# A fused attention, FFN and gated-convolution kernel: batches 2 and 3 row by row, W decode scratch moved, the order replanned

## The chip, the core and the metric

The kernel runs on one core of a Trainium2 chip. A core has five engines, each with its own in-order instruction queue: TensorE (PE, matmuls and weight loads), VectorE (DVE), ScalarE (ACT), GpSimd (POOL) and SyncE (SP), which here only issues DMAs. The metric is the device time of one execution in microseconds. Three runs of the kernel before gave 767.53, 768.31 and 769.16 us, median 768.31.

## The reference

Four batches of 576 positions, 8 heads of 64, model width 512, FFN width 2048:

```
q_rot, k_rot = rotate(q), rotate(k)              # rotary embedding
attn = softmax(q_rot @ k_rot^T / 8)              # per batch and head, 576 x 576
x = heads joined of attn @ v                     # (4, 576, 512)
xn = (x - mean) / sqrt(var + 1e-6) * g_ln
x = x + relu(xn @ w_ch1) @ w_ch2                 # 512 -> 2048 -> 512
gate = sigmoid(causal depthwise conv of x, 5 taps)
out = (gate * (x @ w_val)) @ w_out
```

The weights arrive as 64-bit floats, in 1 MB pieces that are decoded on the chip from their two 32-bit halves. Matmuls that must be accurate split an operand into a high and a low float16 (or two rounded float32) and add three products.

## The kernel before

**Attention.** Work is cut in *score tiles* of 128 queries of one head: 144 of them, 36 for each batch. A tile is: scores on TensorE (`a_scores`, two heads of a pair together), row maximum on VectorE (`a_max`, L478), exponential and a float16 copy on ScalarE (`a_exp` L484, `a_hi` L490), the rest of the float16 split on VectorE (`a_lo`, L495), a DMA transpose issued by SP (`a_turn`, L500), and 14 matmuls with V on TensorE (`a_pv`, L519 and L522). Since 576 is four and a half times 128, the 64 queries left over of both heads of a pair form one tile of their own, the *lead* (its first tile index is `None`). Queries and keys are rotated on VectorE (`mul`, `add`), then split (`hi` on ScalarE, `lo` on VectorE). V is bounded and split as well: absolute sums on ScalarE (`vabs`), one matmul that spreads them (`vsum`), a maximum and a scale on VectorE (`vmax`), then `vhi`, `vlo`, `vturn`.

Batches 0 and 1 go *row by row*: for a row of queries all four head pairs in turn, then the next row, so that a block of 128 positions is complete, in all heads, early. For that the keys of all four pairs stay in SBUF (`kf` for batch 0, `kx0` for batch 1), and queries of a row are loaded and prepared alone (`cuts` lists the rows). Batches 2 and 3 go pair by pair: a pair's keys and all its queries are loaded and prepared together into one buffer of a ring of two (`kq`), and all nine tiles of the pair follow.

**FFN.** When a block of 128 positions is complete, it is normalised (`ln_a` to `ln_d`, transposed by a DMA), and then goes through the FFN in four quarters of the hidden width: `f1` (48 matmuls, L780), `relu` and `hlo`, `f2` (12 matmuls, L808). There are 18 blocks, so 72 `f1` and 72 `f2` steps. `f1` needs W1, which is scaled in four parts of two pieces each; `f2` needs W2, of which the scale is known only when all eight pieces have been decoded.

**Weights.** A 1 MB piece of W is loaded into a scratch buffer (L612), decoded by two ScalarE passes (`p1`, `p0`) and one of VectorE (`p2`, L625), multiplied with itself for a bound (`products`, L641), and, when the scale of its part is known (`conv_max`, `conv_turn`, `conv_scale`), split in two float16 parts (`conv_hi` L679 on ScalarE, `conv_lo` L682 on VectorE, which writes half of `wall`). W1 has three scratch buffers inside `wall`, W2 has two (`kk`), in the space where the ring `kq` lies later. Each `conv_hi` waits for the `conv_lo` before it.

**Last stage.** For pairs of blocks: a transposing DMA, the convolution (`gate_b`), `val` (12 matmuls), `proj` (24), and the store. It begins when the attention buffers are given back.

**Order.** Nothing is ordered at run time. Each piece of work is a `plan.step` with an engine, an assumed duration, a rank, the steps it waits for and the ring buffers it takes or uses. `Plan.run` walks through them with assumed lags (`LAG`) and an assumed DMA rate (`RATE`) and, on each engine, takes the step with the lowest rank among those that can start; that list is the order in which each engine's queue is written. A change of any duration, lag or dependence can so reorder all queues.

Of the kernel before, what the change touches and what calls it, by code (L numbers as in the profile page):

```python
# [27 lines left out]
QS, QK_LEAD_1 = 3, 6  # L28
XT, KQ, RAW, GT, X3, GV = 3, 2, 3, 6, 1, 1
# [125 lines left out]
def kernel(ctx: ExitStack, tc: tile.TileContext, qk, v, g_ln, w_ch1, w_ch2, w_val, conv_w, w_out, rope, eye, out):  # L155
# [40 lines left out]
    kx0 = xpool.tile([128, NP, 2, S], F32R, name="kx0", tag="x1")  # L196
# [27 lines left out]
    ap_k = R(sA, "ap_k", KQ)  # L224
    kk = [ap_k.tile([128, 4 * S], F32, name="kk", tag="kq") for _ in range(2)]
# [59 lines left out]
    attention, early = [], []  # L285
# [4 lines left out]
    def plan_prep(p):  # L290
# [6 lines left out]
        r0 = first[p] - (QK_LEAD_0 if p < NP else QK_LEAD_1 if b < 2 else QK_LEAD)  # L297
# [6 lines left out]
        def vload():  # L304
            st["vt"] = (pool if p < NP else ap_v).tile([128, 10, D], F32, name="vt", tag="vt", bufs=2 if p < NP else 1)
# [50 lines left out]
        for n in ((0,) if two else (1, 0)):  # L356
# [6 lines left out]
            if n:  # L363
                takes = [Buf("kq" if b > 1 else f"kx{pr}" if b else f"kf{pr}")]
                bf["kq"] = takes[0]
            elif b < 2:
                takes = [Buf("qx" if p < NP else "qs" if b else "qf")]
                bf["q"] = takes[0]
            else:
                bf["q"] = bf["kq"]  # L370
# [9 lines left out]
            uses = [bf["raw", n]] + ([bf["q"]] if not n and not takes else [])  # L380
# [709 lines left out]
```

## Time and profile before

| | |
|---|---|
| median of 3 runs | 768.31 us |
| the profiled execution | 765.1 us |
| its span | 763.3 us |
| TensorE busy | 683.1 us, 89% |
| VectorE busy | 621.5 us, 81% |
| ScalarE busy | 454.4 us, 60% |
| DMA moved | 103.60 MB |

The span runs from the first to the last instruction of the profiled execution. What lies around it is 765.1 - 763.3 = 1.8 us. A busy engine is one that executes instructions; matmuls overlap in the pipeline, so a row of matmuls takes less than their number times their mean.

### The profile page before, as it was taken

To read this page: it belongs to the slowest core of one execution; us is meant where nothing else is said; L and a number is where in the kernel's file an instruction comes from. 1 tells how busy PE (TensorE), PEld (TensorE's weight loads), DVE (VectorE), ACT (ScalarE), POOL (GpSimd) and SP (SyncE) were. 2 spreads that over 40 slices of the span, in tenths; PEclk is the share of its full clock that TensorE was granted. 3 is DMA by queue.
4 is the path that set the end of the run, shared out by engine and by line. 5 is a ranking of instruction groups with operands and counts; after the bars stand their busy time and mean duration, and the time that the engine had idled before them with its cause. 6 is when DMAs were issued, how large, how long until landed. Compare 5 with 4: busy or idle time off the path is not lost.

```text
span 763.3 us, 19105 instructions
## 1 busy us (share of the span) xinstructions
PE 683.1 (89%) x7929; PEld 529.0 (69%) x7929; DVE 621.5 (81%) x1257; ACT 454.4 (60%) x778; POOL 16.3 (2%) x40
## 2 busy tenths in 40 slices
PE   2575766789999999999999989999999999999996
PEld 1344645545887777777777767877777887878875
DVE  6889987999889999897787987668779988666525
ACT  5877777787666557776666666464744443333323
POOL 0000000000000000000000100001000000000000
PEclk9977989889999999999999999999999999999999
DMA  8998799754987898689777777768843223301011
GB/s 295 272 249 244 153 244 216 185 126 119 157 138 136 169 186 172 131 170 176 112 149 152 143 139 97 108 114 106 234 70 70 57 56 56 57 29 28 15 56 41
DMA packets 231734, 103.60 MB, mean 136 GB/s; under 512 B 210784, under 2 KB 218976, under 8 KB 231648
## 3 DMA queue, kind: packets, MB, share of 16 engines
q1 hardware_dynamic: 231648, 102.39, 66.4%
q8 instruction: 62, 1.02, 0.6%
q14 instruction: 24, 0.20, 0.1%
HBM read 45.73 MB, written 4.72 MB: 66 GB/s over the span
## 4 chain that ended last, share of the span: by engine, by line
PE 57%; DVE 22%; DMA 13%; ACT 5%; issue 3%; SPq 1%; ACTq 0%; DVEq 0%
PE acc L808 17%; PE hp L780 16%; DMA pT<-p 9%; PE pv L957 6%; PE po L984 6%; PE sc L473 4%; DVE p L495 3%; PE ov L519 3%; DVE nmx L478 3%; PE sc L468 2%; DMA vt<-in_v_dram 2%; DVE wall L682 2%; DVE raw L314 2%; PE ov L522 2%; DVE wall L625 1%
## 5 line engine op out<-in xcount | busy, mean ns | idle before, releaser
L780 PE MATMUL hp<-xT,wall 128*128 128x128 f16 x3456 | 206.0, 220 | 1.6 <-DVE wall L682 1.6
L780 PEld LDWEIGHTS <-wall 128*128 128x128 f16 x3456 | 196.6, 98 | 7.3 <-DVE wall L682 1.8
L808 PE MATMUL acc<-wall,hh 128*128 128x512 f16 x544 | 162.1, 380 | 0.4 <-DVE x L812 0.4
L484 ACT ACTIVATE p<-sc,nmx 128x576 f32<-128x576 f32 x144 | 105.2, 736 | 82.5 <-DVE nmx L478 80.9
L495 DVE SCALAR_TENSOR_TENSOR p<-p,p 128x576 f16<-128x576 f32 x144 | 107.6, 753 | 27.5 <-ACT p L490 27.2
L519 PE MATMUL ov<-vh,pT 128*128 128x65 f16 (+1 forms) x1296 | 93.7, 200 | 27.3 <-DMA pT<-p 17.1
L519 PEld LDWEIGHTS <-pT 128*128 128x128 f16 x1296 | 79.2, 100 | 45.5 <-DMA pT<-p 28.3
L478 DVE TENSOR_REDUCE nmx<-sc 128x1 f32<-128x576 f32 x144 | 105.0, 750 | 4.1 <-PE sc L473 3.6
L808 PE MATMUL acc<-wall,hl 128*128 128x512 f16 x272 | 103.1, 379 | 0.0
L490 ACT ACTIVATE p<-p 128x576 f16<-128x576 f32 x144 | 97.2, 681 | 6.1 <-DMA pT<-p 3.6
L808 PEld LDWEIGHTS <-hh 128*128 128x128 f16 x544 | 48.6, 98 | 51.3 <-issue 2.3
L944 DVE SCALAR_TENSOR_TENSOR gt<-xT,cw,gt 128x256 f32<-128x256 f32 (+4 forms) x192 | 72.1, 413 | 6.6 <-ACT gt L935 4.0
L522 PE MATMUL ov<-vl,pT 128*128 128x64 f16 (+1 forms) x720 | 68.9, 200 | 0.0
L792 ACT ACTIVATE hh<-hp 128x512 f16<-128x512 f32 x68 | 40.1, 590 | 36.7 <-PE hp L780 36.6
L798 DVE SCALAR_TENSOR_TENSOR hl<-hp,hh 128x512 f16<-128x512 f32 x68 | 46.7, 686 | 16.3 <-ACT hh L792 16.2
L522 PEld LDWEIGHTS <-pT 128*128 128x128 f16 x720 | 53.4, 100 | 4.2 <-issue 0.3
L808 PEld LDWEIGHTS <-hl 128*128 128x128 f16 x272 | 26.6, 98 | 32.9 <-DVE hl L798 1.1
L984 PE MATMUL po<-woh,gv 128*128 128x512 f32 x144 | 47.7, 400 | 1.8 <-DVE gv L972 1.4
L957 PE MATMUL pv<-xh,wvh 128*128 128x256 f32 x144 | 44.1, 307 | 0.0
L314 DVE TENSOR_TENSOR raw<-raw,rope_sb 128x1152 f32<-128x1152 f32 (+2 forms) x40 | 39.6, 991 | 4.3 <-DMA raw<-in_qk_dram 4.3
L957 PE MATMUL pv<-xl,wvh 128*128 128x256 f32 x144 | 40.6, 282 | 0.7 <-DVE xl L929 0.7
L957 PE MATMUL pv<-xh,wvl 128*128 128x256 f32 x144 | 40.5, 281 | 0.0
(126 smaller groups left out, 937.6 us busy)
## 6 DMA issues: line engine op xcount, KB each, us to landing
raw<-in_qk_dram SPq DMA_DIRECT2D x24, 576.0 KB, 4.8
wall<-in_moe_w_ch_dram SPq DMA_DIRECT2D x8, 1024.0 KB, 6.5
kk<-in_moe_w_ch_dram SPq DMA_DIRECT2D x8, 1024.0 KB, 6.4
vt<-in_v_dram SPq DMA_DIRECT2D x16, 320.0 KB, 3.6
out_dram<-x SPq DMA_DIRECT2D x18, 256.0 KB, 2.0
raw<-in_qk_dram SPq DMA_DIRECT2D x24, 128.0 KB, 3.1
pT<-p SPq DMA_TRANSPOSE x144, 3.6
r<-in_moe_w_val_dram SPq DMA_DIRECT2D x4, 512.0 KB, 4.7
```

What stands on the lines that cost most here:

```text
L314: nc.vector.tensor_tensor(out=a, in0=a, in1=t, op=ALU.mult)
L478: nc.vector.tensor_reduce(out=nmx, in_=sc[:, :, 0:HS], axis=AX.XY, op=ALU.max, negate=True)
L484: nc.scalar.activation(out=p32.rearrange("p (e n) -> p e n", e=2), in_=sc[:, :, 0:HS], func=ACTF.Exp, bias=nmx)
L490: nc.scalar.activation(out=p16[:, 0], in_=p32, func=ACTF.Copy, scale=P_SCALE)
L495: nc.vector.scalar_tensor_tensor(out=p16[:, 1], in0=p32, scalar=P_SCALE, in1=p16[:, 0], op0=ALU.mult, op1=ALU.subtract)
L519: nc.tensor.matmul(o, pT[:, c], vh[:, 2 * c + hs:2 * c + hs + nh], start=(c == 0), stop=(c == 8))
L522: nc.tensor.matmul(o[..., 0:D], pT[:, c], vl[:, 2 * c + hs:2 * c + hs + nh], start=False, stop=False)
L780: nc.tensor.matmul(hp[:, j], w1[:, u, wl * 512 + o:wl * 512 + o + 128], xT[:, xl * KD + c], start=(i == 0), stop=(i == 3 * KD - 1))
L808: nc.tensor.matmul(st["acc"], lw[:, j], w2[:, f + j, lo * 512:lo * 512 + 512], start=(f + j == 0 and i == 0), stop=(f + j == KF - 1 and i ...
L944: nc.vector.scalar_tensor_tensor(out=gt[:, c0:c1], in0=xT[:, c, HALO + c0 - s:HALO + c1 - s], scalar=col(KT - 1 - s, c), in1=gt[:, c0:c1], ...
L957: nc.tensor.matmul(pv, lw[:, d, c * 128:(c + 1) * 128], rx[:, d], start=(n == 0), stop=(n == 3 * KD - 1))
L984: nc.tensor.matmul(po, lw[:, d, sl], rx[:, d, :], start=(n == 0), stop=(n == 3 * KD - 1))
```

## The change

- Batches 2 and 3 are cut in rows as batches 0 and 1 are (`cuts` by `b % 2`). Their keys lie in `k2`, two tiles of two pairs each in the space of `kk`; each pair's keys are a ring of one (`k20` to `k23`), written for batch 2 and again for batch 3. Their queries use the small ring `qs`.
- W1's scratch: four buffers in `wall` and two in a new tile `xw`, which lies where `kx0` and later the second half of `x` come. W2's: the two `kk` and the same two in `xw`. So `kx0` starts only when the W2 pieces in `xw` are decoded, `k2` when those in `kk` are.
- A `conv_hi` of W1 no longer waits for the `conv_lo` just before it but for the one before that.
- The bounds of V of the four pairs of batch 0 are merged: four absolute sums, four matmuls into one tile, one maximum and one scale for all; their loads have a buffer each (`vt0=NP`).
- `X3` becomes 2 (two buffers for the split block of the last stage), `RATE` 280 in place of 313, the lag of DMA 2.4 in place of 1.9, and several assumed durations change.

On the instructions: the number of matmuls is the same. VectorE has 108 instructions more, ScalarE 24, SP 24 DMAs.

```diff
-XT, KQ, RAW, GT, X3, GV = 3, 2, 3, 6, 1, 1
+T_LAG, RATE, NEAR, AHEAD = 2.4, 280.0, 0.15, 2.0
+XT, KQ, RAW, GT, X3, GV = 3, 2, 3, 6, 2, 1
...
-        if b == 0:
+        if b % 2 == 0:
             cuts = [(c, c + 128, [(0, c), (1, c)]) for c in (0, 128, 256)] + [(384, S, [(None, c4), (0, 384), (1, 384)])]
-        elif b == 1:
+        else:
             cuts = [(0, 192, [(None, c4), (0, 64), (1, 64)])] + [(c, c + 128, [(0, c), (1, c)]) for c in (192, 320, 448)]
-        else:
-            cuts = [(0, S, [(None, c4)] + [(h, f0 + 128 * j) for j in range(4) for h in range(2)])]
...
+        def vsum0():
+            v0["va"] = ps_h.tile([128, NP, 128], F32, name="va0", tag="hp")
+            for j in range(NP):
+                nc.tensor.matmul(v0["va"][:, j], upper(v0["vb"][:, j:j + 1]).to_broadcast([128, 128]), ident, start=True, stop=True)
+
+        def vmax0():
+            vm = pro_x.tile([128, NP], F32, name="vm0", tag="vm0", bufs=1)
+            nc.vector.tensor_reduce(out=vm, in_=v0["va"], axis=AX.X, op=ALU.max)
...
+            v_abs.append(plan.step(ACT, act(640) + 0.09, r, vabs, after=[x0, x1], uses=[vt, vh], row="vabs"))
...
+                x = plan.step(PE, 0.3, R_TINY, vsum0, after=v_abs + [c_c], takes=[hp])
...
+    def k2_start():
+        k2.extend(ap_k.tile([128, 2, 2, S], F32R, name="k2", tag="kq") for _ in range(2))
...
     scratch = (
-        [unit(wfu, a, 4) for a in (18, 22, 26)],
-        [unit(k, 0, 4) for k in kk],
+        [unit(wfu, a, 4) for a in (18, 22, 26, 30)] + [xw[:, 0], xw[:, 1]],
+        [unit(k, 0, 4) for k in kk] + [xw[:, 0], xw[:, 1]],
     )
...
-                    y = plan.step(ACT, act(n) + 0.09, r, lambda a=a: conv_hi(*a), after=[x, chain])
-                    chain = plan.step(DVE, dve(n) + 0.06, r, lambda a=a: conv_lo(*a), after=[y, chain])
+                    y = plan.step(ACT, act(n) + 0.09, r, lambda a=a: conv_hi(*a), after=[x, chains[-1 if w else -2]])
+                    chains.append(plan.step(DVE, dve(n) + 0.06, r, lambda a=a: conv_lo(*a), after=[y, chains[-1]]))
...
+    e_kx = plan.step("", 0, 0, kx_start, after=[p2s[1, 6], p2s[1, 7]])
+    e_k2 = plan.step("", 0, 0, k2_start, after=[p2s[1, 4], p2s[1, 5]])
```

SP's queue around the last W2 loads, before. `kk` rows are W2 pieces, `pT` rows transposes of score tiles, `raw` rows queries or keys, `xT` a normalised block:

```order
L500 DMA_TRANSPOSE pT<-p_1280 128x9x128
L770 DMA_TRANSPOSE xT<-x_1295 128x8x128
L302 DMA raw<-in_qk_dram 128x1152
L500 DMA_TRANSPOSE pT<-p_1322 128x9x128
L612 DMA kk<-in_moe_w_ch_dram 128x2x1024
L500 DMA_TRANSPOSE pT<-p_1339 128x9x128
L500 DMA_TRANSPOSE pT<-p_1443 128x9x128
L612 DMA kk<-in_moe_w_ch_dram 128x2x1024
L500 DMA_TRANSPOSE pT<-p_1464 128x9x128
L302 DMA raw<-in_qk_dram 128x2x192
L500 DMA_TRANSPOSE pT<-p_1564 128x9x128
L612 DMA kk<-in_moe_w_ch_dram 128x2x1024
```

And in the changed kernel, where W2's pieces lie in `kk` and `xw` in turn:

```order
L304 DMA raw<-in_qk_dram 128x2x192
L531 DMA_TRANSPOSE pT<-p_921 128x9x128
L649 DMA kk<-in_moe_w_ch_dram 128x2x1024
L531 DMA_TRANSPOSE pT<-p_942 128x9x128
L304 DMA raw<-in_qk_dram 128x2x192
L649 DMA xw<-in_moe_w_ch_dram 128x2x1024
L531 DMA_TRANSPOSE pT<-p_1031 128x9x128
L531 DMA_TRANSPOSE pT<-p_1064 128x9x128
L304 DMA raw<-in_qk_dram 128x2x192
L649 DMA xw<-in_moe_w_ch_dram 128x2x1024
```

Each piece ends with the last W2 load. Before, 25 score transposes stand ahead of it in the queue, and 3 ahead of the first W2 load; in the changed kernel 16 and 8.

VectorE's queue up to the first W2 piece that is split (`wall<-wall,s`), before. `wn`, `w_m`, `w_r` and `scl` belong to W2's bound and scale, `nmx` and `p` to score tiles, `vl` to V, `raw` to keys and queries:

```order
L478 TENSOR_REDUCE nmx<-sc 128x1
L657 TENSOR_REDUCE wn_1925<-hp 128x1
L147 TENSOR_SCALAR w_m<-wn_1925 128x1
L148 RECIPROCAL w_m<-w_m 128x1
L150 TENSOR_SCALAR w_r<-w_m 128x1
L668 TENSOR_SCALAR s_77<-srt,w_r 128x4
L644 TENSOR_SCALAR scl<-w_r 128x1
L670 TENSOR_SCALAR scl<-scl,smin 128x1
L429 SCALAR_TENSOR_TENSOR vl<-vt,sv,vh 128x640
L322 TENSOR_TENSOR raw<-raw 128x192
L314 TENSOR_TENSOR raw<-raw,rope_sb 128x1152
L682 SCALAR_TENSOR_TENSOR wall<-wall,s_77 128x2x512
```

And in the changed kernel, where `rd` and `x` belong to the end of an attention group:

```order
L573 TENSOR_TENSOR x_67<-ov,rd 128x128
L526 SCALAR_TENSOR_TENSOR p_1421<-p_1411,p_1421 128x576
L694 TENSOR_REDUCE wn_1435<-hp 128x1
L148 TENSOR_SCALAR w_m<-wn_1435 128x1
L149 RECIPROCAL w_m<-w_m 128x1
L151 TENSOR_SCALAR w_r<-w_m 128x1
L705 TENSOR_SCALAR s_77<-srt,w_r 128x4
L681 TENSOR_SCALAR scl<-w_r 128x1
L707 TENSOR_SCALAR scl<-scl,smin 128x1
L526 SCALAR_TENSOR_TENSOR p_1433<-p_1430,p_1433 128x576
L509 TENSOR_REDUCE nmx<-sc 128x1
L719 SCALAR_TENSOR_TENSOR wall<-wall,s_77 128x2x512
```

The piece has moved ahead of the first V and the first keys of batch 1. It stands behind 25 row maxima and 24 `a_lo`, where it stood behind 31 and 30.

## Rows read from the trace of the kernel before

**Rows 1.** The page, busy tenths in 40 slices of 19 us: TensorE and its granted clock.

```profile
PE   2575766789999999999999989999999999999996
...
PEclk9977989889999999999999999999999999999999
```

**Rows 2.** Busy us by engine in five stretches, with granted clock, DMA share and GB/s.

```profile
0.00:125.00 125.00, 73.55 (x818) 55.92 (x820) 105.41 (x223) 89.23 (x128) 2.69 (x12) 0.89 0.96 239
0.00:150.40 150.40, 91.71 (x1062) 70.91 (x1064) 127.77 (x269) 109.21 (x160) 3.41 (x14) 0.90 0.96 234
150.40:172.00 21.60, 17.47 (x114) 9.07 (x111) 20.26 (x32) 18.29 (x29) 0.36 (x2) 0.78 0.55 125
172.00:540.00 368.00, 356.84 (x4852) 274.94 (x4851) 313.70 (x597) 237.17 (x414) 12.57 (x24) 1.00 0.81 143
540.00:763.30 223.30, 217.11 (x1911) 174.07 (x1907) 159.82 (x362) 89.78 (x179) 0.00 (x0) 1.00 0.26 59
```

**Rows 3.** First 200 us by line: duration min/median/max in ns, first and last start.

```profile
L612 SPq DMA_DIRECT2D kk<-in_moe_w_ch_dram x8: 382/525/987, 31.3 to 129.5; - x8
...
L625 DVE SCALAR_TENSOR_TENSOR wall<-wall,kk x8: 1215/1218/1222, 84.3 to 142.6; 128x1024 int32<-128x1024 int32 x8
...
L682 DVE SCALAR_TENSOR_TENSOR wall<-wall,s x8: 1274/1278/1285, 150.4 to 171.1; 128x1024 f16<-128x1024 f32 x8
...
L808 PE MATMUL acc<-wall,x x48: 379/379/631, 154.8 to 174.8; 128*128 128x512 f16 x48
```

**Rows 4.** TensorE's waits in the first 155 us: total us, times, longest.

```profile
PE bound L641 <- DVE wall L625: 15.4, 9, 5.3
...
PE ov L519 <- DMA pT<-p: 10.0, 7, 3.1
```

**Rows 5.** VectorE groups by shape: busy us, mean ns of one, idle before.

```profile
L495 DVE SCALAR_TENSOR_TENSOR p<-p,p 128x576 f16<-128x576 f32 x144 | 107.6, 753 | 27.5 <-ACT p L490 27.2
...
L478 DVE TENSOR_REDUCE nmx<-sc 128x1 f32<-128x576 f32 x144 | 105.0, 750 | 4.1 <-PE sc L473 3.6
...
L798 DVE SCALAR_TENSOR_TENSOR hl<-hp,hh 128x512 f16<-128x512 f32 x68 | 46.7, 686 | 16.3 <-ACT hh L792 16.2
...
L314 DVE TENSOR_TENSOR raw<-raw,rope_sb 128x1152 f32<-128x1152 f32 x24 | 32.4, 1351 | 1.8 <-DMA raw<-in_qk_dram 1.8
...
L314 DVE TENSOR_TENSOR raw<-raw,rope_sb 128x256 f32<-128x256 f32 x12 | 5.0, 417 | 0.0
```

**Rows 6.** Chain that ended last: start us, us, what, for single steps.

```profile
91.70 1.17 PE sc L468 x8
...
139.97 1.33 DVE nmx L478 x2
...
207.56 0.05 PE ov L519
...
208.00 2.68 PE hp L780 x48
...
210.69 0.06 PE ov L519
...
211.48 0.98 PE sc L473 x12
...
212.99 2.59 PE acc L808 x12
```

**Rows 7.** TensorE's timeline at the first second-layer matmuls: start us, us, what.

```profile
154.76 5.31 PE L808 MATMUL acc<-wall,x 128*128 128x512 f16 x12
```

**Rows 8.** The page, DMA issues: count, KB each, us to landing.

```profile
raw<-in_qk_dram SPq DMA_DIRECT2D x24, 576.0 KB, 4.8
...
raw<-in_qk_dram SPq DMA_DIRECT2D x24, 128.0 KB, 3.1
```

**Rows 9.** Timeline of the end: last wait of TensorE, last ScalarE copy.

```profile
754.74 0.50 PE L984 MATMUL po<-woh,gv 128*128 128x512 f32 x1 [1.44 <-DVE gv L972]
...
759.67 0.60 ACT L988 ACTIVATE x<-po 128x512 f32<-128x512 f32 x1 [2.21 <-PE po L984]
```

More of the change, by code (lines that the diff above doesn't have):

```diff
@@ L224 @@
     ap_k = R(sA, "ap_k", KQ)
+    k2 = []
     kk = [ap_k.tile([128, 4 * S], F32, name="kk", tag="kq") for _ in range(2)]
@@ L296, in plan_prep @@
         two = base[p] != p
-        r0 = first[p] - (QK_LEAD_0 if p < NP else QK_LEAD_1 if b < 2 else QK_LEAD)
+        r0 = first[p] - (QK_LEAD_0 if p < NP else QK_LEAD if two else K_LEAD)
         def load(n):
@@ L379, in plan_prep @@
             x = plan.step(DVE, dve(w), r, lambda n=n: add(n), after=[x], uses=[bf["raw", n]])
-            uses = [bf["raw", n]] + ([bf["q"]] if not n and not takes else [])
-            after = [x] + ([bf["hk"]] if b > 1 and not n else [])
+            uses = [bf["raw", n]]
+            after = [x]
             x = plan.step(ACT, act(w), r, lambda n=n: hi(n), after=after, takes=takes, uses=uses, row="hi")
             if n:
-                bf["hk"] = x
+                if b:
+                    kx_homes.append((b, x))
             if not n and ts[0][0] is None:
@@ L440, in plan_prep @@
         x1 = plan.step(POOL, 0.2, r, vabs_m, takes=[vh], row="vh")
+        if p < NP:
+            v_abs.append(plan.step(ACT, act(640) + 0.09, r, vabs, after=[x0, x1], uses=[vt, vh], row="vabs"))
+            v_rest.append((r, vt, vh, vhi, vlo, vturn, bf))
+            if p == NP - 1:
+                x = plan.step(PE, 0.3, R_TINY, vsum0, after=v_abs + [c_c], takes=[hp])
+                x = plan.step(DVE, 1.0, r - 8, vmax0, after=[x], takes=[sv0], uses=[hp])
+                for r, vt, vh, vhi, vlo, vturn, f in v_rest:
+                    h = plan.step(ACT, act(640) + 0.1, r - 8, vhi, after=[x], uses=[vt, vh, sv])
+                    y = plan.step(DVE, dve(640) + 0.05, r - 8, vlo, after=[h], uses=[vt, vh, sv])
+                    z = plan.step(ACT, 1.1, r - 8, vturn, after=[h], uses=[vh])
+                    f["v"] = [y, z]
+                    early.append(y)
+                    attention.extend([y, z])
+            return
         x = plan.step(ACT, act(640) + 0.09, r, vabs, after=[x0, x1], takes=[vb], uses=[vt, vh])
@@ L565 @@
             ss = [Buf("ss") for _ in range(ne)]
[L566 removed]
+            x = plan.step(PE, (1.6 if h is None else 2.2) if b == 0 else 0.9 if h is None else 1.05, R_SC + i, lambda i=i: a_scores(i), after=bf["ready"] + ([bf["dg"]] if h is None else []), takes=ss,
                           uses=([bf["qd"]] if h is None else []) + [vf["kq"], bf["q"]], row="sc")
@@ L684 @@
     w_ready, p2s = {}, {}
-    chain = None
+    chains = [None] * 4
     for w in range(2):
@@ L1012 @@
             x = plan.step(ACT, act(256) + 0.09, r, lambda m=m, c=c: gate_a(m, c), after=[last, cw_step], takes=[gt], uses=[xT], row="gt")
-            x = plan.step(DVE, sum(dve(c1 - c0) + 0.15 for _, c0, c1 in taps(m)), r, lambda m=m, c=c: gate_b(m, c), after=[x], uses=[xT, gt])
+            x = plan.step(DVE, sum(dve(c1 - c0) for _, c0, c1 in taps(m)), r, lambda m=m, c=c: gate_b(m, c), after=[x], uses=[xT, gt])
             g = plan.step(ACT, act(256), r, lambda m=m, c=c: gate_c(m, c), after=[x], uses=[gt])
-            x = plan.step(PE, 1.45, R_VAL + m, lambda m=m, c=c: val(m, c), after=[h, l] + w3["wv"] + ([gate_order] if c else []), takes=[pv], uses=[x3], row="val")
+            x = plan.step(PE, 1.42, R_VAL + m, lambda m=m, c=c: val(m, c), after=[h, l] + w3["wv"] + ([gate_order] if c else []), takes=[pv], uses=[x3], row="val")
             gate_order = x
@@ L1023 @@
             po = Buf("po")
-            x = plan.step(PE, 2.85, R_PROJ + m, lambda m=m, s=s: proj(m, s), after=lasts + w3["wo"], takes=[po], uses=[gv], row="proj")
+            x = plan.step(PE, 2.8, R_PROJ + m, lambda m=m, s=s: proj(m, s), after=lasts + w3["wo"], takes=[po], uses=[gv], row="proj")
             x = plan.step(ACT, act(512), R_PROJ + m, lambda m=m, s=s: proj_a(m, s), after=[x], uses=[po])
```

75 lines of the change are left out of this document (43 added, 32 removed).

## The prediction

> **What bounds the kernel now.** I read the busy slices first: TensorE is between 5 and 7 tenths busy in the first eight slices, some 150 us, and 9 in nearly all that follow, and its granted clock is below full only in those first slices [rows 1]. The stretches put numbers on it. In the first 150.4 us TensorE works 91.7 us; from 172 to 540 it works 356.8 of 368, and from 540 to the end 217.1 of 223.3 [rows 2]. Its work is fixed (the change leaves every matmul), so what is lost stands in the start: 58.7 us idle by 150.4 and 4.1 more until 172, against 11.2 in the long middle and 6.2 at the end.
>
> What holds the start is VectorE, 127.8 us busy of 150.4 [rows 2]. TensorE waits there for decoded pieces of W (15.4 us) and for transposes (10.0) [rows 4]. The work that would fill it is the FFN, and its second half is shut until W2's scale is known: the eight W2 loads are issued from 31.3 to 129.5 us, their last decode starts at 142.6, the first split piece at 150.4 and the first `f2` at 154.8 [rows 3]. Until then only eight `f1` steps can run, since their results have no more room. The loads come that slowly because two scratch buffers serve eight pieces. So the number to forecast is when `f2` starts, and how much TensorE work has been left behind by then.
>
> **W2 earlier (the scratch, the order).** By the two queues, the first W2 piece has less VectorE work ahead of it: 6 row maxima at 0.750 and 6 `a_lo` at 0.753, 9.0 us; 4 `hlo` at 0.686, 2.7 us [rows 5]; the rotation and split of batch 1's first keys and of some queries, about 5.5 us (two rotations of 1.351 [rows 5], the rest narrower); the V bound, scale and split of batch 1's first pair with the three bounds that are merged, about 3.5 us; one block's normalisation and three group ends, about 4.2 us. That is 24.9 us in durations. Neighbours overlap a little: two maxima take 1.33 us in the chain, not 1.50 [rows 6]; I take 0.92, so 22.9 us. VectorE then reaches the piece with 127.8 - 22.9 = 104.9 us of work done, which the kernel before had done at 125.0 us (105.4) [rows 2]. `f2` follows 4.4 us behind the first piece [rows 3]: 129.4.
>
> Two things can delay it. The merged V bounds wait for four V loads where one did; the four loads move up by two pieces' worth of bytes, and I count 0 to 3 us. And the transfers: ahead of the last W2 load now lie 28.4 MB (16 pieces of 1.05, four keys and the table of 0.59, sixteen query rows of 0.13 or 0.20, four V of 0.33, 17 transposes of 0.29). At the 239 GB/s of the first 125 us, with the DMA 0.96 busy [rows 2], they take 119 us; with the decode behind it the last piece would be ready about 5 us later than VectorE's work allows. At the rate of a stretch with more loads and fewer transposes it is no delay. Bounds 0 to 6 us; I take 2.6 for both, since the mix moves towards large loads. `f2` starts at 132.0 us, 22.8 earlier.
>
> **What is left behind.** That is not the gain. Ahead of the first `f2` TensorE does less: 6 `f1` in place of 8 (2.68 each), 24 `a_pv` in place of 30 (four at 0.44, two leads at 0.79), four score steps fewer (1.17 each, as for batch 0; the chain's steps, [rows 6]): 5.4 + 3.3 + 4.7 = 13.4 us that now come later. Net 22.8 - 13.4 = 9.4 us.
>
> **From the first `f2` to the fourth.** The four wait for split pieces. Before, these lie between 150.4 and 171.1 us [rows 3], and TensorE is 17.5 of 21.6 us busy, at a granted clock of 0.78 [rows 2]. In the changed order VectorE has 4.5 us more to do between the first and the last piece, but TensorE has two `f1` and a score step more there, 6.7 us: 2.2 us won.
>
> One price there is not of the order. The first `f2` took 5.31 us, against 2.59 for the same twelve matmuls later [rows 6, 7], in a stretch with a granted clock of 0.78 [rows 2]: it ran at the lower level, 1.2 GHz, after TensorE had waited. The Trainium skill's page "TensorE: Matmul & The Clock Gate" (Part 1: The HAM clock gate) says that the clock falls when the engine has been idle and rises after sustained work; the trace agrees. By the row alone one could book 2.7 us as won if `f2` starts earlier; by the page the slow start would only move with it, since the stretch ahead is as thin, and nothing is won. I book nothing.
>
> **Less slack behind it.** TensorE's gain brings it closer to VectorE. Counted in the queues as above, between score tiles 28 and 48 TensorE has 5 `f1`, 10 `f2` and twenty tiles' scores and V, 64 us; VectorE has twenty maxima and `a_lo`, five W2 pieces, the keys and V of batch 1 and what the FFN needs, 64 us as well. A tile's matmuls with V wait for its transpose behind `a_lo`, so TensorE will meet VectorE there once. I give back 2 us, bounds 0 to 6.
>
> **Batches 2 and 3 row by row.** 32 query rows are prepared apart in batches 2 and 3 where 8 whole pairs were. A narrow rotation costs 0.417 us, a wide one 1.351 [rows 5]; with adds, splits and 24 more group ends VectorE gets some 17 us of work more, nearly all between 250 and 540 us. Between 172 and 540 VectorE idles 54.3 of 368 us [rows 2], which hides it; without that cover it would cost up to 17. The 32 added small loads land in 3.1 us against 4.8 for 4.5 times the bytes [rows 8]; the bytes are the same, and they are issued rows ahead. The skill's page "DMA: Bandwidth & Descriptors" (Bandwidth) has the rule to batch transfers, because small ones reach a small part of the peak; it speaks against this part. By the row nothing is lost, since the DMA has a fifth of that stage free (share 0.81 [rows 2]). An estimate from that page's figures: the 4.7 MB of queries would take 34 us at its 138 GB/s for 64 KB and 14 at its 341 for 1 MB; were the DMA the bound in that stage, the sum would lose those 20 us. I take 0. That blocks become complete sooner is worth 0 to 4 us in that stage; I take 0 of it as well, against the hand-overs between batches, where V and keys now wait for the last row of the batch before (0 to 4 each).
>
> **The end.** TensorE idles 6.2 us from 540 on [rows 2]: 3.6 are the last copy and store from 759.67, 1.4 the wait at 754.74 [rows 9]. The order now puts two `proj` and six `val` behind the last `f2` ahead of its gate, 8 us more cover than before, and a second `X3` buffer. Won 1.5, bounds 0 to 2.4. The relaxed `conv_hi` chain and the changed assumed durations act only through the order, already counted.
>
> **Sum.** 9.4 + 2.2 - 2.0 + 0 + 1.5 = 11.1 us off the span: 763.3 - 11.1 = 752.2. The profiled execution is 1.8 us longer than its span, 754.0, and the median of the runs lies 3.2 us above the profiled one: 757.
>
> **Rivals.**
> - *The DMA holds W2.* If the 28.4 MB go at no more than 239 GB/s and the transposes behind them queue, the last W2 piece is ready about 10 us later than VectorE allows, and transposes, already 10.0 us of TensorE's waits [rows 4], come later too. For it: DMA 0.96 busy [rows 2]. Against: the loads are then spread over four buffers, and only 0.55 busy follows from 150.4 [rows 2]. The gain shrinks to 1 or 2 us: 767.
> - *Hand-overs stall (slower).* Keys of batch 3 go into the buffers of batch 2, and the V buffers turn over only with the last row of a batch. A pair's V takes about 8 us from load to split, four pairs one after another, while a pair gives TensorE two tiles, about 6 us with the FFN between. Where the filled-in FFN steps don't cover it, a hand-over costs up to 16 us; above 6 us at each of the two new ones the gain is gone. Against: the order puts some 8 us of extra FFN into each. At 10 us each: 757 + 20 = 777.
> - *The middle was waiting for blocks.* At tile 108 the old order had used up all 36 `f1` of the nine complete blocks. If much of the 11.2 us idle from 172 to 540 [rows 2] came from that, and the give-back does not come, another 8 us go: 749.
>
> **How the numbers follow.** Forecast 0.57, from the bounds 750 to 764; DMA 0.15; hand-overs 0.12; middle 0.16. What a measurement of this kernel tells from no change is about 0.2%, 1.5 us. Faster: 0.57 + 0.16 and half of the DMA case, 0.79; same 0.07; slower 0.14. The range leaves out most of the hand-overs and the far end of the middle case: 747 to 768.
>
> **What would show it.** The first `f2` within 126 to 140 us, with six `f1` ahead; W2 loads done by about 110. VectorE above 0.95 busy from 130 to 215. TensorE's idle time from 172 to 540 still about 11. If `f2` starts on time and the end does not move by ten, the give-back is mis-sized; if `f2` starts above 145, the DMA case holds. TensorE idle above 6 us at either of the two new batch hand-overs would make the slower case right.

## The result and the profile after

The changed kernel takes 744.0 us (median of 4 runs, 743.6 to 744.15) against 767.9 for the kernel before beside it: ratio 0.9698, 95% interval 0.9658 to 0.9737. The forecast was 757, range 747 to 768: the direction was right, the gain about twice the forecast one. The profiled execution has a span of 741.8 us, 21.5 less than the 763.3 before.

The busy slices of 18.5 us each, to be read against [rows 1]:

```profile
PE   3446879899999999999999999999999989999998
...
PEclk9965878999999999999999999999999998999999
```

TensorE stays at 8 or 9 from the seventh slice on, from 111 us, where before it did so from the ninth, 153 us. The clock is low in the third to seventh slices, from 37 to 130 us. A new dip stands near the end, in slices 33 and 34. Where the 21.5 us came from is best read in four stages cut at the same events: the first `f2`, the first matmul with V of the 72nd score tile (end of batch 1) and of the 144th. First the kernel before, then the changed one (length, busy us of PE, PEld, DVE, ACT, POOL, granted clock, DMA share, GB/s):

```profile
0.00:154.80 154.80, 93.67 (x1080) 71.96 (x1081) 131.53 (x276) 112.47 (x167) 3.59 (x15) 0.88 0.94 229
154.80:302.40 147.60, 143.97 (x1757) 104.42 (x1757) 137.46 (x279) 99.93 (x177) 4.52 (x10) 0.98 0.81 153
302.40:528.20 225.80, 216.57 (x3043) 169.58 (x3040) 184.52 (x323) 147.08 (x247) 6.58 (x12) 1.00 0.79 134
528.20:763.30 235.10, 228.91 (x2064) 183.03 (x2060) 168.05 (x382) 94.97 (x189) 1.64 (x3) 1.00 0.29 65
```

The same view of the changed kernel:

```profile
0.00:124.60 124.60, 78.18 (x873) 61.96 (x874) 110.77 (x224) 96.00 (x133) 2.90 (x12) 0.81 1.01 259
124.60:296.40 171.80, 167.22 (x2088) 123.41 (x2085) 159.28 (x336) 122.02 (x217) 6.12 (x13) 0.99 0.79 146
296.40:530.60 234.20, 231.43 (x3219) 181.46 (x3216) 203.53 (x443) 152.91 (x272) 7.36 (x14) 1.00 0.76 136
530.60:741.80 211.20, 204.22 (x1768) 164.35 (x1764) 157.56 (x365) 88.40 (x181) 0.55 (x1) 0.98 0.27 68
```

Length minus PE busy is TensorE's idle time: 61.1, 3.6, 9.2 and 6.2 us before; 46.4, 4.6, 2.8 and 7.0 after. So 14.7 us come from the start, 6.4 from the third stage (batches 2 and 3), 2.1 from less busy time for the same work (683.1 to 681.0), and 1.8 are lost in the second and the last stage. The first block's four `f2`, busy 13.6 us before and 11.2 after, account for it; the mean granted clock of the whole span is not higher, 0.961 against 0.973.

The stretches that answer to [rows 2]; the first ends at the issue of the last W2 load, the second at the first split W2 piece, and the third is the last 8.7 us ahead of that piece:

```profile
0.00:95.90 95.90, 54.39 (x555) 42.13 (x556) 84.32 (x170) 76.80 (x105) 1.95 (x11) 0.80 1.04 280
0.00:119.00 119.00, 72.58 (x774) 56.87 (x775) 105.23 (x216) 93.08 (x129) 2.90 (x12) 0.80 1.04 268
110.30:119.00 8.70, 8.70 (x97) 7.36 (x97) 8.15 (x22) 5.54 (x9) 0.00 (x0) 0.72 0.96 207
119.00:124.60 5.60, 5.60 (x103) 5.09 (x101) 5.53 (x10) 2.92 (x4) 0.00 (x0) 1.00 0.39 76
119.00:145.00 26.00, 23.64 (x249) 16.24 (x247) 25.47 (x45) 19.17 (x30) 0.73 (x2) 0.95 0.56 103
172.00:540.00 368.00, 365.06 (x5058) 285.62 (x5056) 320.77 (x706) 240.21 (x428) 12.94 (x24) 1.00 0.78 141
540.00:741.80 201.80, 194.82 (x1630) 156.76 (x1627) 154.53 (x356) 87.00 (x178) 0.00 (x0) 0.98 0.26 64
```

The DMA moved 280 GB/s while W2's loads were issued, where the row that the forecast used has 239; VectorE had 105.2 us of work ahead of the first split piece, as forecast (104.9), but did it by 119.0 us, not by 125. Loads and pieces, to be read against [rows 3] (count, min/median/max ns, first to last start; the start of a load is its issue on SP, and the decode of the last one begins at 103.3 us):

```profile
L649 SPq DMA_DIRECT2D xw<-in_moe_w_ch_dram x6: 463/486/582, 37.6 to 95.8; - x6
L649 SPq DMA_DIRECT2D kk<-in_moe_w_ch_dram x4: 367/420/572, 55.2 to 84.0; - x4
```

```profile
L719 DVE SCALAR_TENSOR_TENSOR wall<-wall,s x8: 1273/1278/1285, 119.0 to 143.7; 128x1024 f16<-128x1024 f32 x8
```

The first `f2`, in TensorE's timeline (start, us), to be read against [rows 7]:

```profile
124.61 2.75 PE L852 MATMUL acc<-wall,x 128*128 128x512 f16 x12
```

It starts at 124.6 us (forecast 132) and takes 2.75 us, not 5.31: the granted clock had been 1.00 from 119.0 on. Ahead of the first `f2` of the kernel before it was 0.57, with TensorE busy 5.5 of 9.7 us:

```profile
145.00:154.70 9.70, 5.49 (x53) 4.13 (x52) 8.77 (x24) 7.54 (x14) 0.18 (x1) 0.57 0.45 95
```

TensorE's waits in the first 155 us, against [rows 4]:

```profile
PE bound L678 <- DVE wall L662: 12.6, 9, 3.2
...
PE ov L550 <- DMA pT<-p: 4.9, 4, 2.0
```

And VectorE's own waits up to its first split W2 piece (total us, times, longest), before and then after:

```profile
DVE rd L537 <- PE ov L519: 6.2, 6, 2.6
...
DVE raw L314 <- DMA raw<-in_qk_dram: 2.8, 2, 2.5
```

```profile
DVE rd L568 <- PE ov L550: 1.0, 2, 0.8
```

VectorE waits for group ends 1.0 us in place of 6.2, and for keys 0.3 in place of 2.8; that is 7.7 of the 8.8 us by which its idle time up to the piece fell (22.6 to 13.8). The matmuls of a group end wait in turn for transposes, 10.0 us of TensorE's waits before and 4.9 after. TensorE's waits from 155 us to the end, before:

```profile
PE ov L519 <- DMA pT<-p: 7.1, 8, 1.9
```

And after; the waits for transposes went from 7.1 us in 8 to 1.3 in 2:

```profile
PE acc L852 <- DVE gt L988: 2.1, 1, 2.1
...
PE acc L852 <- DVE hl L842: 1.5, 4, 0.6
...
PE ov L550 <- DMA pT<-p: 1.3, 2, 0.8
```

VectorE's narrow rotations, to be read against [rows 5]: 36 in place of 12, at the same duration, and 16 wide ones in place of 24:

```profile
L316 DVE TENSOR_TENSOR raw<-raw,rope_sb 128x1152 f32<-128x1152 f32 x16 | 21.6, 1349 | 0.3 <-DMA raw<-in_qk_dram 0.3
L316 DVE TENSOR_TENSOR raw<-raw,rope_sb 128x256 f32<-128x256 f32 x36 | 14.9, 414 | 0.0
```

The small loads, to be read against [rows 8]; they land no later than before:

```profile
raw<-in_qk_dram SPq DMA_DIRECT2D x16, 576.0 KB, 4.4
raw<-in_qk_dram SPq DMA_DIRECT2D x48, 128.0 KB, 2.8
```

The `gv` wait of 1.44 us at the end of [rows 9] is gone; the last copy on ScalarE is still 0.60 us long; ScalarE had stood idle 2.20 us until the last matmul let it start:

```profile
738.19 0.60 ACT L1032 ACTIVATE x<-po 128x512 f32<-128x512 f32 x1 [2.20 <-PE po L1028]
```

### The profile page after: what moved, and what is told of

Its sections match the earlier page's. It is cut to its first block, busy times and chain, and to the rows that moved or that the text cites. A ratio compares the mean times of both kernels' runs of the same rounds, so it can differ in the third digit from the quotient of the medians.

```text
span 741.8 us, 19303 instructions
## 1 busy us (share of the span) xinstructions
PE 681.0 (92%) x7929; PEld 531.2 (72%) x7929; DVE 631.1 (85%) x1365; ACT 459.3 (62%) x802; POOL 16.9 (2%) x40
## 4 chain that ended last, share of the span: by engine, by line
PE 56%; DVE 28%; ACT 7%; DMA 5%; issue 3%; SPq 0%; ACTq 0%; DVEq 0%
PE hp L824 16%; PE acc L852 16%; PE po L1028 6%; PE sc L504 5%; DVE gt L988 4%; PE pv L1001 4%; PE ov L550 4%; DVE p L526 4%; DVE nmx L509 3%; DMA pT<-p 3%; DVE raw L316 2%; PE ov L553 2%; ACT p L521 2%; ACT p L515 2%; DVE hl L842 2%
## 5 line engine op out<-in xcount | busy, mean ns | idle before, releaser
L852 PE MATMUL acc<-wall,hh 128*128 128x512 f16 x544 | 163.8, 383 | 2.1 <-DVE gt L988 2.1
L550 PE MATMUL ov<-vh,pT 128*128 128x65 f16 (+1 forms) x1296 | 94.8, 201 | 10.9 <-DMA pT<-p 6.2
L550 PEld LDWEIGHTS <-pT 128*128 128x128 f16 x1296 | 80.4, 100 | 25.3 <-issue 10.6
L553 PEld LDWEIGHTS <-pT 128*128 128x128 f16 x720 | 53.9, 101 | 4.1 <-issue 0.4
L992 ACT ACTIVATE gt<-gt 128x256 f32<-128x256 f32 x36 | 15.0, 417 | 54.9 <-DVE gt L988 54.9
L316 DVE TENSOR_TENSOR raw<-raw,rope_sb 128x256 f32<-128x256 f32 (+2 forms) x64 | 43.1, 673 | 0.3 <-DMA raw<-in_qk_dram 0.3
L1001 PE MATMUL pv<-xh,wvh 128*128 128x256 f32 x144 | 42.2, 293 | 0.0
```

The source lines that it names most:

```text
L550: nc.tensor.matmul(o, pT[:, c], vh[:, 2 * c + hs:2 * c + hs + nh], start=(c == 0), stop=(c == 8))
L553: nc.tensor.matmul(o[..., 0:D], pT[:, c], vl[:, 2 * c + hs:2 * c + hs + nh], start=False, stop=False)
L852: nc.tensor.matmul(st["acc"], lw[:, j], w2[:, f + j, lo * 512:lo * 512 + 512], start=(f + j == 0 and i == 0), stop=(f + j == KF - 1 and i ...
L1001: nc.tensor.matmul(pv, lw[:, d, c * 128:(c + 1) * 128], rx[:, d], start=(n == 0), stop=(n == 3 * KD - 1))
```

## The experiments

All are the changed kernel with the edit named, but for two, which are the kernel before with a part added. Of a long line the diffs show only the part that changes. Ratios are to the kernel before in the same set of runs; its medians go from 764.3 to 767.9 over the sets, and the changed kernel was run in the first alone, so a difference of less than about 0.5% between two edited kernels rests on their traces, one execution each. Idle is TensorE's in the four stages of above, from the same view of each kernel's profile; "busy" is TensorE's, the same work in each.

| kernel | median us | ratio, 95% | span | first `f2` | idle by stage | busy |
|---|---|---|---|---|---|---|
| before | 767.9 | 1 | 763.3 | 154.8 | 61.1, 3.6, 9.2, 6.2 | 683.1 |
| changed | 744.0 | 0.966-0.974 | 741.8 | 124.6 | 46.4, 4.6, 2.8, 7.0 | 681.0 |
| W2 in two buffers | 756.2 | 0.983-0.990 | 752.6 | 144.8 | 55.2, 6.8, 1.7, 9.2 | 679.8 |
| before + W2 buffers | 757.2 | 0.985-0.993 | 758.7 | 135.1 | 52.0, 8.4, 10.7, 5.9 | 681.8 |
| V bounds apart | 747.4 | 0.972-0.979 | 744.2 | 127.6 | 48.9, 5.5, 3.1, 7.3 | 679.4 |
| chain as before | 742.0 | 0.966-0.973 | 739.4 | 124.6 | 48.2, 5.5, 2.0, 8.2 | 675.6 |
| old numbers, all | 748.2 | 0.972-0.981 | 746.2 | 130.3 | 47.7, 6.0, 5.5, 5.3 | 681.7 |
| old DMA numbers | 759.0 | 0.985-0.994 | 756.9 | 131.5 | 51.1, 8.0, 5.4, 9.0 | 683.4 |
| before + numbers | 772.5 | 1.005-1.011 | 770.6 | 142.2 | 50.8, 10.9, 1.5, 19.4 | 688.0 |
| pairs | 758.6 | 0.986-0.993 | 755.8 | 124.5 | 46.9, 4.9, 2.1, 18.7 | 683.2 |
| pairs, old numbers | 766.9 | 1.000-1.004 | 765.8 | 132.3 | 48.9, 5.3, 11.9, 11.6 | 688.0 |
| pairs, old end numbers | 747.2 | 0.972-0.979 | 745.7 | 124.0 | 44.2, 5.0, 2.3, 11.4 | 682.9 |
| two buffers, old numbers | 771.0 | 1.005-1.011 | 769.4 | 150.7 | 50.7, 6.1, 8.1, 11.6 | 692.9 |
| X3 = 1 | 756.4 | 0.983-0.993 | 755.8 | 123.4 | 44.6, 4.5, 2.6, 15.9 | 688.1 |
| X3 = 1, old end numbers | 743.8 | 0.967-0.974 | 742.9 | 124.3 | 45.1, 4.5, 2.8, 8.8 | 681.7 |
| old gate number | 736.4 | 0.957-0.964 | 736.2 | 125.3 | 46.8, 4.7, 2.9, 3.7 | 678.0 |
| old end numbers | 736.3 | 0.959-0.966 | 733.9 | 124.0 | 45.3, 4.7, 2.1, 3.7 | 678.1 |
| old end numbers, chain | 735.5 | 0.957-0.962 | 733.2 | 125.8 | 43.3, 5.6, 2.0, 3.7 | 678.6 |

### The start: W2's buffers, the V bounds, the chain

The W2 pieces in the two `kk` only (two buffers in place of four), with the order of loads and the starts of `kx0` and `k2` that go with it:

```diff
-        [unit(k, 0, 4) for k in kk] + [xw[:, 0], xw[:, 1]],
+        [unit(k, 0, 4) for k in kk],
```

> The changed kernel with W2's pieces in the two kk buffers alone (W1 keeps its six). Theory S, that four W2 buffers bring the second layer forward: VectorE work ahead of the first split W2 piece goes from 105.5 to 119.5 us by the queue, so the first f2 moves from 124.6 to about 139, with 8 f1 ahead in place of 6; lost time there rises by some 4 us and the kernel takes 748 us (745 to 752). Rival N, that the new durations and lags in the planner made the gain: no change, 744. If all of the start's gain hangs on it: 757 or more.

Measured 756.2: later than either theory, and just short of the last answer (757). The first `f2` comes 20 us later, 8.8 us of idle return in the start, and the span is 10.8 longer. So the buffers are worth about 11 us here. Then the buffers alone, in the kernel before. With this line and `xw` come W1's three further buffers, and the later query rows of batches 0 and 1 are prepared with a lead of 8 places, not 6:

```diff
-        [unit(k, 0, 4) for k in kk],
+        [unit(k, 0, 4) for k in kk] + [xw[:, 0], xw[:, 1]],
```

> The kernel before with one part of the change alone, W2 pieces in the six buffers of xw as well. VectorE's work ahead of the first split W2 piece falls from 128.1 to 114.9 us, TensorE's ahead of the first f2 from 68.7 to 62.0. Theory S, additive: the first f2 starts some 15 us sooner (140), 9 to 11 us are kept to the end, 754 to 758. Rival G (an early start with the old DMA numbers is given back in the middle and the last stage, as when the W2 buffers, V merge and X3 were there without rows and numbers): the first f2 is as early, the loss at the last projection is 104 to 110, 763 to 770.

757.2, as the additive theory had it: by its interval 5 to 12 us are kept. The trace is that of its slowest execution (760.5). In it the start gains 9.1 us of idle and the second and third stage lose 6.3; the rival's give-back is real and takes part of it.

No run undoes W1's buffers or the lead by themselves. With both of them, but two W2 buffers, the first `f2` comes at 144.8 us; the kernel before with the new numbers, which has neither, is at 142.2. So nothing shows that they bring it forward without W2's. Next, the merged bounds and the relaxed chain:

```diff
-        if p < NP:
-            sv = sv0
...
-        if p < NP:
+        if False:
             v_abs.append(plan.step(ACT, act(640) + 0.09, r, vabs, after=[x0, x1], uses=[vt, vh], row="vabs"))
```

> The changed kernel with batch 0's V bounds taken pair by pair again, two V buffers. By the prediction the merge costs 0 to 3 us of start and saves 1.9 us of VectorE: 744, within 2 us either way. If the merge removed waits that count (TensorE stood 7.2 us for V bounds in the first 155 us of the kernel before): 748 to 751.

747.4, between the two answers. By the traces the merge is worth 2.5 us of idle at the start, and the span is 2.4 shorter with it; the intervals of the two ratios overlap.

```diff
-after=[x, chains[-1 if w else -2]])
+after=[x, chains[-1]])
```

> The changed kernel with one edit undone: a weight piece is again made behind the piece just before it, not the one two back. The forecast put no price on it. By the rows: VectorE's work ahead of the first split W2 piece 103.4 in place of 105.5 us, 7 f1 in place of 6 ahead of the first f2, so a first f2 within 3 us of 124.6. If that is all it does: 742 to 748. If the edit is what lets VectorE go on without idling (13 us idle ahead of that piece in place of 22): f2's first start falls back to 130 us or later, and 748 to 754.

742.0, at the ratio of the changed kernel, and the first `f2` at the same 124.6: this edit is not what let VectorE go on.

### The middle: the planner's numbers

```diff
-T_LAG, RATE, NEAR, AHEAD = 2.4, 280.0, 0.15, 2.0
+T_LAG, RATE, NEAR, AHEAD = 1.9, 313.0, 0.15, 2.0
...
-(1.6 if h is None else 2.2) if b == 0 else 0.9 if h is None else 1.05
+(1.1 if h is None else 1.45) if b == 0 else 0.85 if h is None else 1.08
...
-sum(dve(c1 - c0) for _, c0, c1 in taps(m))
+sum(dve(c1 - c0) + 0.15 for _, c0, c1 in taps(m))
```

> The changed kernel with the planner's old numbers (DMA lag 1.9, rate 313, old durations of scores, f1, f2, val, proj, taps). Theory N, that the new numbers make the middle's gain, because transposes are now planned as late as they come: TensorE's waits for transposes return from 6 to about 17 us and the kernel takes 752 us. Theory R: 744 to 746.

748.2, between the two answers: the first `f2` is 5.7 us later and 2.7 us of idle return in the third stage, but the last stage loses less (5.3 against 7.0). Numbers for the middle and numbers for the end pull apart, so they were split. The DMA's alone, the first line of that diff and the planned time of a transpose with it:

> The changed kernel with only the DMA numbers of the planner as before: lag of a transpose 1.9 in place of 2.4, rate 313 in place of 280, time of a turn as before. If these are what took the waits on p's transposes out of the middle: about 6 us of such waits come back after 155 us, and the loss at pair 144 is 85 to 88 in place of 78.4, total 748 to 752. If the durations of the TensorE and score steps did it: the loss at pair 144 stays at 78 to 80 and the total at 743 to 746.

759.0, more than either answer: 15 us of span for the assumed DMA times. The first `f2` is 6.9 later and every stage is idle for longer. This is what let VectorE go on at the start. It reaches the first split piece at 126.3 us with nearly the same work done (106.7 us for 105.2) but 19.6 us idle in place of 13.8. Its own wait for group ends is back, and so is TensorE's for transposes (both up to that piece):

```profile
DVE rd L568 <- PE ov L550: 6.4, 4, 3.0
...
PE ov L550 <- DMA pT<-p: 15.5, 8, 7.0
```

After 155 us TensorE's waits for transposes return too, 4.0 of the 8.0 us by which the three later stages are idle for longer:

```profile
PE ov L550 <- DMA pT<-p: 5.3, 10, 1.3
```

With the old numbers the planner counts 1.9 us of lag and 1.05 for the transfer, 2.95, with the new 3.45. The trace of the changed kernel gives the landing after the issue, and the new number fits it:

```profile
pT<-p SPq DMA_TRANSPOSE x144, 3.5
```

Lag, rate and transpose time were changed together, so what each is worth is not shown. Then all new numbers in the kernel before:

> The kernel before, with nothing of the change but the planner's new numbers (lag of a transpose 2.4, rate 280, the new durations of the score, f1, f2, gate, value and projection steps). Theory N (the numbers are worth what the middle gained, since the changed kernel with the old numbers lost 7.5 us between pair 40 and the end of the attention): TensorE's idle time from pair 72 to pair 144 falls from 11.4 us to about 4, with few waits of transposes on the DMA of p; the first f2 comes about 7 us earlier (VectorE work ahead of the first split W2 piece 120 instead of 128 us). For the last stage, theory M (these numbers misplan a last stage whose blocks come pair by pair, and that is what the pairs experiment lost): about 18 us idle there, as in the pairs experiment, so 762 us in all. Theory R (what the pairs experiment lost at the end is owed to something else of the change, X3 or the key rings): the last stage stays at 6 us idle, 750 us in all.

772.5, slower than before (1.005 to 1.011) and than either theory. The third stage is idle 1.5 us in place of 9.2, as theory N had it, and the second 10.9 in place of 3.6, which no theory had; busy time grew by 4.9. And the last stage lost what theory M said, mostly in these waits:

```profile
PE pv L957 <- ACT xh L924: 6.9, 2, 6.5
PE pv L957 <- DVE xl L929: 6.2, 6, 2.2
```

### The last stage: rows, numbers, X3

Batches 2 and 3 cut in pairs again, with the ring `kq`:

```diff
-        if b % 2 == 0:
+        if b > 1:
+            cuts = [(0, S, [(None, c4)] + [(h, (64 if b % 2 else 0) + 128 * j) for j in range(4) for h in range(2)])]
+        elif b % 2 == 0:
```

> The changed kernel with batches 2 and 3 pair by pair again (ring kq, queries with their keys). Theory R, that the middle gained (idle time of TensorE from score tile 72 to 144 fell by 8 us) because blocks are complete sooner: the idle time comes back and the kernel takes 751 us (749 to 754). Rival N, the planner's numbers: no change, 744, or up to 2 less, since VectorE has 17 us less to do.

758.6, more than either theory. Until the 144th tile nothing is lost: idle 53.9 us against 53.8. Row by row gives nothing in the batches where it is done. Of the 14 us of span 11.7 are idle time in the last stage, mostly in these waits, and 2.2 are busy time:

```profile
PE pv L1007 <- ACT xh L974: 6.5, 1, 6.5
PE acc L858 <- ACT hh L842: 3.2, 2, 2.5
PE acc L858 <- DVE hl L848: 3.0, 2, 2.3
```

Was that the pairs, or an order planned with wrong numbers? Pairs with all old numbers, pairs with those of gate, value and projection alone ("old end numbers"), and rows with all old numbers and two W2 buffers:

> The changed kernel with batches 2 and 3 pair by pair and with the planner's old numbers. The middle is to lose 7 to 8 us, as with the old numbers and rows. Theory M (the pairs experiment lost 14 us at the end because the new numbers misplan it): the last stage is idle for about 6 us as in the kernel before, and the span comes to 746 to 749 us, level with the old numbers and rows (746.2). Theory R' (row by row is what shortens the last stage, whatever the numbers): the last stage is idle for some 15 to 19 us, and the span is 758 to 764.

> The changed kernel with batches 2 and 3 pair by pair, and three groups of the planner's numbers, those of the gate, value and projection steps, which lie for the most part in the last stage, as before (0.15 us more for a group of gate taps, 1.45 and 2.85). The middle should keep the new numbers' gain (loss at pair 144 near 78.5). Theory M with these three as its cause: the last stage is idle for about 6 us, span 743 to 746. If M's cause is in other numbers, or R' holds: still 15 to 19 us idle, span 753 to 757.

> The changed kernel without its six W2 buffers in xw and without its planner's numbers: what is left is the rows, the merged V bounds, the chain and X3. If the gains add up: 10.8 us from the W2 buffers and 4.4 from the numbers are gone, so 759 us in all (span 757), and the rest (rows, V merge) is worth the 9 us that remain to 768. If without the two nothing is left, since an early start that the middle or the end doesn't keep is given back: 764 to 768.

766.9, 747.2 and 771.0; the first and the third are above every answer. The second has theory M's span (743 to 746), but 11.4 us idle in the last stage, not about 6. And as shown below, rows gain 8 us from the same old end numbers, so of the 14 us between pairs and rows these numbers explain about 2; 11.8 remain.

The 6.5 us wait for `xh` stays in all three, and it isn't the pairs': the third has rows. What the five kernels with this wait share is their order: behind the last `f2` TensorE has only 4 `val` and 2 `proj` left, all of one pair of blocks (a `proj` here is one step of 12 matmuls; a pair of blocks has two). It waits while that pair's transposing DMA (3.05 us) and its copies run. From the last `f2` to the end there are 25.8 us in these pairs as in the kernel before, which has 5 `val` and 4 `proj` there; what TensorE lacks of work, it idles (first the kernel before, then the pairs with old end numbers):

```profile
737.45:763.30 25.85, 19.66 (x108) 15.47 (x107) 14.39 (x30) 8.53 (x18) 0.00 (x0) 1.00 0.16 51
```

```profile
719.90:745.70 25.80, 14.49 (x72) 12.07 (x72) 13.56 (x28) 7.02 (x15) 0.00 (x0) 0.80 0.11 30
```

That is 6.2 us idle, all that the last stage of the kernel before has, and 11.3 of 11.4. In the five kernels the idle time behind the last `f2` is 11.1 to 11.7 us; in the changed kernel, with 7 `val` and 6 `proj` there, it is 3.7. In no trace with 5 `val` and 4 `proj` or more is a single wait for `xh` longer than 1.8 us. No run changes this number of steps by itself.

The third of these kernels was also to tell whether gains add up: they don't. Without W2's further buffers and the numbers nothing of the rest is left (771.0 against 764.3 beside it). Next, rows with the old end numbers, then with the gate's alone:

```diff
-sum(dve(c1 - c0) for _, c0, c1 in taps(m))
+sum(dve(c1 - c0) + 0.15 for _, c0, c1 in taps(m))
...
-plan.step(PE, 1.42, R_VAL
+plan.step(PE, 1.45, R_VAL
...
-plan.step(PE, 2.8, R_PROJ
+plan.step(PE, 2.85, R_PROJ
```

> The changed kernel with the planner's numbers of the gate, value and projection steps as before (0.15 us more for a group of gate taps, 1.45 and 2.85); lag, rate and the other durations as changed. The pairs experiment with these three was 10 us faster than without, and its whole gain lay in the last stage. Theory M2 (the new three misplan the last stage with rows too): the loss after pair 144, 8.2 us in the changed kernel, falls to the 4 us that the old numbers gave, and the time is 738 to 741. Rival: with rows the last stage has work in hand either way, and the time stays at 743 to 746. Either way the loss at pair 144 stays near 78.5.

> The changed kernel with only the number of a group of gate taps as before (0.15 us more). If this number is the cause of the last stage's loss: as e9, 735 to 738, loss after pair 144 1 to 3 us. If the value and projection numbers are: 742 to 746, loss near 8.

736.3 and 736.4: better than the changed kernel by about 1%, and the number of the gate alone does it (the 0.15 us is for each tap instruction, not for a group of them). The trace of the changed kernel shows that its own number was the wrong one: it plans a tap of 256 columns at 0.34 us, the old number at 0.49, and it takes 0.48:

```profile
L988 DVE SCALAR_TENSOR_TENSOR gt<-xT,cw,gt 128x256 f32<-128x256 f32 x80 | 38.6, 483 | 4.9 <-ACT gt L979 2.8
```

In the changed kernel VectorE is full from 600 to 620 us and TensorE waits behind taps, for `gt` and `hl`; first that stretch of the changed kernel, then of the one with the old end numbers:

```profile
600.00:620.00 20.00, 17.23 (x117) 12.31 (x116) 19.89 (x57) 7.66 (x17) 0.00 (x0) 0.83 0.26 56
```

```profile
600.00:620.00 20.00, 20.00 (x189) 17.67 (x189) 18.61 (x53) 8.97 (x19) 0.00 (x0) 1.00 0.21 54
```

2.8 us idle, and the granted clock is 0.83 with it. In the second kernel the chain of its last 34 us (start, us, what) has no wait but the last copy:

```profile
703.39 5.61 PE po L1028 x24
709.00 8.55 PE pv L1001 x72
717.55 5.61 PE po L1028 x24
723.16 1.41 PE pv L1001 x12
724.57 5.62 PE po L1028 x24
...
730.22 0.60 ACT x L1032
```

The second buffer for the split block, with the new and with the old end numbers:

```diff
-XT, KQ, RAW, GT, X3, GV = 3, 2, 3, 6, 2, 1
+XT, KQ, RAW, GT, X3, GV = 3, 2, 3, 6, 1, 1
```

> The changed kernel with one buffer of the third kind (X3) in place of two, as before. Nothing before the last stage should differ (first f2 124.6, loss at pair 144 78.4). If X3 feeds the end: the loss after pair 144 grows from 8.2 by several us, 747 to 752. If not: 742 to 746.

> Both X3 = 1 and the gate, value and projection numbers as before. If the second X3 buffer is worth its 14 us by itself: 748 to 752 (loss after pair 144 about 15). If X3's loss was, like the pairs', a last stage misplanned by the new three numbers: 736 to 739.

756.4 and 743.8: it is worth 12 us with the new numbers, more than expected, and 7.5 with the old end numbers, between the two answers. Without it `val` waits for the split block, with the new numbers:

```profile
PE pv L1001 <- DVE xl L973: 9.3, 6, 3.0
PE pv L1001 <- ACT xh L968: 2.9, 2, 1.8
```

Last, the old end numbers and the old chain together:

> The chain as before and the gate, value and projection numbers as before. The chain as before gained 2.9 us by pair 144 and lost 0.9 of it in the last stage. If the last stage is idle 1 to 2 us as with these numbers alone: loss at the last projection 77, time 734 to 735. If the earlier work is given back: 736 to 738.

735.5, the fastest median; the intervals of this kernel (0.957 to 0.962) and of the old end numbers alone (0.959 to 0.966) overlap, so the chain is worth nothing that these runs can tell.

## Why the prediction was wrong

- **The sum.** Booked were 9.4 us for the start, 2.2 - 2.0 for the second stage, nothing for the third and 1.5 for the end. In idle time 14.7, -1.0, 6.4 and -0.8 came, and 2.1 less busy time.
- **The mechanism of the start held, its size did not.** Six `f1` ahead of the first `f2`, VectorE's work ahead of the first split piece (105.2 for 104.9), W2's last load issued at 95.8 us: as forecast. The mis-sized term is the time at which VectorE gets through that work: 119.0 us, not 125.0, since I let it idle as long as before (20 us; it was 13.8), and no delay came from DMA or V (2.6 booked); `f2` followed 5.6 us behind the piece, not 4.4. It came 30.2 us earlier, not 22.8. TensorE had done 15.5 us less by then (78.2 for 93.7), not 13.4, so 14.7 net, not 9.4. With the old DMA numbers VectorE idles 19.6 us ahead of the piece, `f2` comes at 131.5, close to my 132, and the start is worth 10.0: what I left out is what these numbers do to the waits ahead of it.
- **"The relaxed chain and the changed assumed durations act only through the order, already counted"** is the step that failed, for the durations; the chain is worth nothing that these runs can tell. The order was counted for work, not for waits. With the old DMA numbers 4.7 us of idle return in the start, 6.0 in the second and third stage and 2.0 in the last, 15 us of span with the busy time; the gate's number costs 6 to 8. These prices don't add up: all old numbers together cost 4.4 us of span, and all new ones make the kernel before slower.
- **The middle, taken at nothing,** gave 6.4 us of idle in the third stage. The rival "the middle was waiting for blocks" had the size (749), but not the cause: with pairs the third stage is idle 2.1 us, with rows 2.8. What brings idle time back there is old numbers: the second and third stage together idle 7.4 us in the changed kernel, 13.4 with the old DMA numbers, and 12.8 before. The numbers need the rest of the change for it: in the kernel before the new ones leave 12.4.
- **Row by row cost nothing, as booked** (its work on VectorE, 13.5 us and not 17 against the pairs, is hidden), **but it goes with 12 to 14 us of span,** under either set of end numbers. I had looked for its use in the batches where it is done. With the old end numbers all 7.7 us of the difference in idle time in the last stage (11.4 against 3.7) lie behind the last `f2`.
- **The end:** 1.5 won was forecast; 0.8 us more idle came. The 1.44 us wait for `gv` went as said, and behind the last `f2` 2.5 us were won. But 3.3 us of waits behind the gate's taps came ahead of it.
- **The first `f2`'s slow clock** was booked as moving with it, as the Trainium skill's rule on the clock ("TensorE: Matmul & The Clock Gate", Part 1: The HAM clock gate) seemed to have it here. It didn't: the first `f2` took 2.75 us, 2.6 less, with a granted clock of 1.00 in the 5.6 us ahead of it. The rule isn't against that; my reading that the stretch ahead would be as thin was wrong: from 110.3 us to the first `f2` TensorE was busy throughout (8.70 of 8.7 and 5.60 of 5.6 us), where before it was busy 5.5 of the last 9.7.
- **The other rivals:** the DMA didn't hold W2 (280 GB/s at a share of 1.04, where I feared 239), and hand-overs didn't stall (2.8 us idle in all of the third stage).
- **The signs** missed on the fast side: the first `f2` came before 126 us, TensorE idled 2.9 us from 172 to 540 and not 11, and VectorE was 0.92 busy from 130 to 215, not above 0.95.
- **Smaller terms:** two `f1` and a score step are 6.5 us by the prediction's prices, not 6.7. And the step from the profiled execution to the median, 3.2 us before, was 0.4 after: 2.8 of the 13 us between 757 and 744.

What stays open: why old numbers bring so much idle time to the third stage with pairs (11.9 us) or two W2 buffers (8.1) against 5.5 with rows and four; and what W1's buffers, the lead of the queries, and the lag and the rate are worth apart. Each change rewrites most of the order, and I have not followed these to an instruction.

## What to carry to other kernels

Where a planner writes the order, its assumed durations are part of the change: compare each with the trace (a transposing DMA's landing by its measured median, 3.5 us here, where 2.95 was planned; a tap by its 0.48) and try them alone, since they can outweigh the edit they come with. Count what an earlier start frees in the waits of the engine that feeds it, not in its work alone. And see that enough TensorE work of other blocks stands behind the last `f2`, where a chain of 25.8 us with a DMA in it runs to the end: with 5 `val` and 4 `proj` 6.2 us of it were idle, with 4 and 2 over 11.

## What the runs showed of the hardware

With `X3 = 1` idle time in the last stage was paid nearly twice: TensorE idles 8.9 us more there than in the changed kernel, and over the span it is busy 7.1 us more with the same matmuls; its mean granted clock is 0.95 against 0.961. It is not always so: the pairs idle 11.7 us more there and are busy 2.2 us more. Behind the last `f2`, 4 `val` and 2 `proj` took 14.5 us of busy time at a granted clock of 0.80; by the chain of the kernel with old end numbers, where nothing waits, the same steps take 11.3 (two thirds of 8.55, and 5.61). Over all runs the same work took from 675.6 to 692.9 us of busy time. And the DMA carried W2's large loads among transposes at 280 GB/s in the first 95.9 us, where the kernel before moved 244 in the same time.
